# Batch 0's mirrored rows through device memory and gathers, its folds behind a chunk of batch 1: a lightning attention and Fourier mixing kernel

## The chip, the cores and the metric

The kernel runs on one core of a Trainium2 chip. Its time is the device time of one execution in microseconds. A core has five engines that run side by side, each with its own queue in a fixed order: TensorE (PE: matmuls and transposes into PSUM; its weight loads are shown as PEld), VectorE (DVE), ScalarE (ACT), GpSimd (POOL) and SyncE (SP), which here only starts DMAs. ACT and POOL start DMAs too.

## What is computed

Two stages, from the reference:

```
# attention, blocks of 64 positions, decay lam per head
intra = (qb @ kb.T * Dmask) @ vb
inter = (qb * lam_pow) @ kv_state
out[block] = intra + inter
kv_state = lam_block * kv_state + (kb * rev_pow).T @ vb
# bridge: x[b, s, h*D + d] = out[b, h, s, d]
mixed = real(fft(fft(x, axis=1), axis=2))
u = x + mixed
un = (u - mean(u)) / sqrt(var(u) + 1e-6)
result = u + relu(un @ w_ch1) @ w_ch2
```

There are 4 batches, 8 heads, 768 positions and 64 elements a head, so x has rows of 512 for each batch; w_ch1 is 512 x 2048 and w_ch2 2048 x 512. Both weights come as 64-bit floats and are converted on the chip.

## The kernel before

**Attention** (`attn`, L246) runs per batch over six chunks of 128 positions. `attn_in` (L259) loads q, k and v on SP's queue, multiplies k by the decay on POOL (kd, L270), transposes k and q on TensorE (L274, L279), copies them out on ACT and scales q on DVE (L285). `attn_out` (L289) forms the scores (L298), masks them on DVE (sc, L302), forms the state's increment (L315, then L319 on POOL and L320 on DVE) and the output transposed (L328, L332), which ACT copies to oT. The inner `back` (L345) transposes four tiles of it (L348) and copies two halves (L350, L351) to rows x, the second half of the columns reversed.

**Folds and Fourier.** The real part of the transform is made from sums and differences of row s and row S - s, so each batch needs its rows in mirrored order too. `fold_a` (L448) uses rows 384 to 576 and their mirror, `fold_b` (L452) the others; both are DVE work in place, the first two operations of each fold placed in program order on their engine (L418, L419). Then `fft_ln` (L483) runs the matmuls over the positions (L508), whose first one is placed in program order too, the matmuls over the width (L521 to L526), adds x, normalises (L534) and, for the first four groups, transposes the result to ut, the operand of the MLP. Groups of two row tiles are taken in the order 1, 2, 0.

**Mirrored rows.** There are two ways. For a batch in `TURNED`, only batch 0, `attn_out` copies the output with its positions reversed (L386; one column apart, L339, L341, L392), and `mirrored` (L374) passes it through `back` a second time. For the other batches x goes to two device memory tensors, xa and xb, on ACT's queue (L358, L360, L362), and `mirror_a` (L425, three gathers) and `mirror_b` (L441, two) fetch the rows in mirrored order by indirect DMAs from POOL.

**Order.** Every part is a Python generator that yields an estimate of its time; `weave`, `beside` and `part` interleave them, which gives the order in which the program is written. The framework's scheduler may move an instruction within its engine's queue from there. From L833 on: attention 0 runs with 8 of the 32 tiles of weights (each a load of 512 KB and five DVE and two ACT operations, L216 to L225); then the fold of batch 0 beside 2.5 chunks of attention 1; then the Fourier part of batch 0 beside 3.5 chunks and 4 weight tiles; then halves of the MLP (L625, L639) beside the rest of the weights and the fronts of batches 1 to 3. After 438 us of the profile come the last eight groups' products, joined in pairs (L712, L759). `LEADS = (0,)` lets attention 1 begin before batch 0's Fourier part.

Buffers that bear on it: x tiles of chunks 3 to 5 come from a pool of three (`xn`), those of chunks 0 to 2 and the mirrored tiles from one of twelve (`xp`), q, k and v from two each, PSUM tiles of the front from five.

Of the kernel before, what the change touches and what calls it, by code (L numbers as in the profile page):

```python
# [76 lines left out]
def kernel(  # L77
# [61 lines left out]
    def new(pool, shape, tag, **kw):  # L139
        cnt[0] += 1  # L140
        return pool.tile(shape, F32, tag=tag, name=f"{tag}{cnt[0]}", **kw)
# [87 lines left out]
    def weights():  # L229

        for h in range(2):
            for f in range(h * DFF // 2, (h + 1) * DFF // 2, WP):
                for c in range(KO):
                    load_weights(w1[:, c, f:f + WP], w1v[:, c, f:f + WP])
                    yield 1.0
            for c in range(h * FO // 2, (h + 1) * FO // 2):
                load_weights(w2[:, c, :], w2v[:, c, :])
                yield 1.0
# [7 lines left out]
    def attn(b):  # L246

        head = () if b - 1 in LEADS else attn_in(b, 0)
        for c in range(NC):
            yield from head  # L250
            head = attn_in(b, c + 1) if c < NC - 1 else attn_in(b + 1, 0) if b in LEADS else ()
            yield from attn_out(b, c, head)

    ins, oTs, eo = {}, {}, {}
    LEADS = (0,)
    TURNED = (0,)
    first = const.tile([128, HP, 1], F32, name="first")

    def attn_in(b, c):  # L259
# [29 lines left out]
    def attn_out(b, c, head):  # L289
# [45 lines left out]
        nc.scalar.copy(oT, po)  # L335
        if b in TURNED:

# [14 lines left out]

        if b not in TURNED:
            x = xn_[b, c] = new(xp, [C, DM], "x") if c < HC else new(xn, [C, DM], "xn")
# [126 lines left out]
    T_FOLD = 2 * (2 * 2.2 + 4 * 0.8)  # L481
# [314 lines left out]
    def weave(lead, other, ratio):  # L796

        t_lead = t_other = 0.0
        for d in lead:
            t_lead += d  # L800
            while t_other < t_lead * ratio:
                d = next(other, None)
                if d is None:
                    return t_lead + sum(lead)
                t_other += d
                yield d
            yield d
        return t_lead

    def run(gen):  # L810
        return sum(gen)

    def part(gen, n):
        for d in gen:
            yield d
            n -= d
            if n <= 0:
                return
# [5 lines left out]
    NW = 2 * KO * DFF // WP  # L824
    w = weights()
    t_chunk = 7.3
# [3 lines left out]
    def beside(lead, t, other, t_other):  # L830
        return weave(lead, part(other, t_other), t_other / t)

    att1, mix = attn(1), fft_ln(0)  # L833
# [1 line left out]
    run(part(att0, 2.7))  # L835
    run(beside(att0, NC * t_chunk - 2.7, w, 0.25 * NW))

    run(beside(part(mix, T_FOLD), T_FOLD, att1, 2.5 * t_chunk))
    run(beside(mix, 24.0, beside(att1, 3.5 * t_chunk, w, 0.12 * NW), 0.12 * NW + 2.5 * t_chunk))

    half = [[mlp(b, g, h * FO // 2, (h + 1) * FO // 2) for b, g in PLAIN[:3]] for h in range(2)]
    fr = chain([att1, fft_ln(1)] + [front(b) for b in range(2, B)])
# [52 lines left out]
```

## Time and profile before

| | |
|---|---|
| median of 6 runs | 831.65 us (830.02 to 833.84) |
| profiled execution | 831.25 us |
| its span, first to last instruction | 829.1 us |
| TensorE idle from 0 to 130 us | 20.6 us |
| mean granted TensorE clock | 0.996 |
| DMA moved | 68.87 MB |

All lines come from the profiled execution. A line of the timeline has the start and the length in us (or, for several merged, from the first to the last), the engine, the line of the source, the operation, what it writes and reads, and in brackets how long the engine was idle before and what it waited for. A q after an engine's name stands for its queue: the issue of a DMA, not its transfer. The chain of waits goes back from the last instruction to what released each step. Durations of single operations overlap by some 0.08 us on DVE and by more on TensorE, so in a full queue starts are closer than durations.

### The profile page before, as it was taken

What the parts mean: (1) busy time and instruction counts of PE and PEld (TensorE: products, weight loads), DVE (VectorE), ACT (ScalarE), POOL (GpSimd) and SP (SyncE); (2) the same over time, 40 slices, a digit from 0 to 9 for tenths busy, and PEclk for the clock granted to TensorE, in tenths of its full rate; (3) what the DMA queues carried; (4) which work ended last, traced back from release to release, by engine and by line L of the source; (5) the groups of instructions that cost most, each with busy time, mean ns of one, the idle gap of its engine ahead of it and who ended that gap; (6) DMA issues with size and microseconds to landing.
All of it is one profiled execution on the core that took longest, in us unless ns stands there. A gap on an engine that the chain in (4) does not pass through costs nothing.

```text
span 829.1 us, 11682 instructions
## 1 busy us (share of the span) xinstructions
PE 798.7 (96%) x4608; PEld 635.8 (77%) x4608; DVE 443.4 (53%) x1030; ACT 182.9 (22%) x436; POOL 79.1 (10%) x102
## 2 busy tenths in 40 slices
PE   6989889999999999999999999999999999999998
PEld 5767765758675857767748888888888888888886
DVE  6889788847943572355894551156313561145411
ACT  4755433215420210312102210022001210012100
POOL 3121140012110110220100000000000000000000
PEclk9999999999999999999999999999999999999999
DMA  9966633256950137430442011100111001100010
GB/s 248 257 148 179 165 110 98 72 135 169 248 150 27 51 61 156 115 132 3 115 123 80 1 52 51 51 1 0 52 51 51 0 1 39 33 32 1 1 39 25
DMA packets 126683, 68.87 MB, mean 83 GB/s; under 512 B 111150, under 2 KB 112174, under 8 KB 126630
## 3 DMA queue, kind: packets, MB, share of 16 engines
q1 hardware_dynamic: 121488, 55.67, 26.2%
q0 software_dynamic: 2112, 6.69, 2.4%
q10 hardware_dynamic: 3030, 5.78, 1.9%
q8 instruction: 36, 0.59, 0.3%
q14 instruction: 17, 0.14, 0.1%
HBM read 48.72 MB, written 19.40 MB: 82 GB/s over the span
## 4 chain that ended last, share of the span: by engine, by line
PE 80%; DVE 10%; issue 4%; DMA 3%; ACT 2%; POOL 1%; POOLq 0%; DVEq 0%; ACTq 0%
PE p L759 23%; PE p L712 23%; PE pm L639 10%; PE pm L625 7%; PE pa L508 3%; PE pa L332 3%; PE pa L298 3%; PE pa L328 2%; DMA x<-xb,ix 1%; PE pa L274 1%; PE pa L315 1%; PE pa L348 1%; DVE stt L538 1%; DMA xb<-xn 1%; PE pa L279 1%
## 5 line engine op out<-in xcount | busy, mean ns | idle before, releaser
L625 PE MATMUL pm<-ut,w 128*128 128x256 f32 x512 | 119.1, 382 | 0.2 <-DVE hr L631 0.2
L639 PE MATMUL pm<-w,hr 128*128 128x512 f32 x256 | 117.7, 604 | 1.3 <-DVE hr L631 1.3
L625 PEld LDWEIGHTS pm<-ut,w 128*128 128x128 f32 x512 | 94.4, 190 | 15.4 <-issue 3.1
L712 PE MATMUL p<-ur,w 128*128 128x256 f32 x384 | 93.8, 379 | 0.0
L639 PEld LDWEIGHTS pm<-w,hr 128*128 128x128 f32 x256 | 47.2, 192 | 51.3 <-issue 47.7
L712 PEld LDWEIGHTS p<-ur,w 128*128 128x128 f32 x384 | 73.0, 190 | 10.3 <-issue 0.5
L712 PE MATMUL p<-us,w1s 128*128 128x256 f32 x256 | 65.7, 379 | 0.0
L759 PE MATMUL p<-w,hs 128*128 128x256 f32 x256 | 58.0, 379 | 0.5 <-DVE y L780 0.5
L759 PE MATMUL p<-w2s,hs 128*128 128x256 f32 x256 | 57.9, 379 | 0.0
L759 PE MATMUL p<-w,ha 128*128 128x256 f32 x256 | 57.9, 379 | 0.0
L759 PEld LDWEIGHTS p<-w,hs 128*128 128x128 f32 x256 | 48.5, 190 | 7.5 <-DVE y L780 0.9
L759 PEld LDWEIGHTS p<-w2s,hs 128*128 128x128 f32 x256 | 48.6, 190 | 6.6
L712 PEld LDWEIGHTS p<-us,w1s 128*128 128x128 f32 x256 | 48.6, 190 | 6.6
L759 PEld LDWEIGHTS p<-w,ha 128*128 128x128 f32 x256 | 48.6, 190 | 6.6
L614 POOL DMA_INDIRECT out_dram<-y,ix x12 | 11.9, 988 | 408.1 <-DVE y L785 343.7
L739 ACT COPY ha<-p 128x256 f32<-128x256 f32 x32 | 11.9, 372 | 169.1 <-PE p L712 169.1
L332 PE MATMUL pa<-sc,v 128*64 128x128 f32 x384 | 32.3, 286 | 5.6 <-DVE sc L302 5.6
L750 DVE TENSOR_TENSOR ha<-p,ha 128x256 f32<-128x256 f32 x32 | 13.6, 425 | 44.8 <-ACT ha L749 44.8
L302 DVE TENSOR_TENSOR sc<-pa,decay 128x512 f32<-128x512 f32 x48 | 31.4, 683 | 11.0 <-PE pa L298 10.8
L298 PEld LDWEIGHTS pa<-qT,kT 64*128 64x128 f32 x384 | 26.1, 193 | 12.2 <-ACT qT L281 5.4
L332 PEld LDWEIGHTS pa<-sc,v 128*64 128x64 f32 x384 | 23.5, 140 | 14.5 <-DVE sc L302 9.5
L298 PE MATMUL pa<-qT,kT 64*128 64x128 f32 x384 | 30.8, 292 | 2.6 <-ACT qT L281 2.3
(144 smaller groups left out, 1133.2 us busy)
## 6 DMA issues: line engine op xcount, KB each, us to landing
raw<-in_moe_w_ch_dram SPq DMA_DIRECT2D x32, 512.0 KB, 4.9
k<-in_k_dram SPq DMA_DIRECT2D x24, 256.0 KB, 4.8
q<-in_q_dram SPq DMA_DIRECT2D x24, 256.0 KB, 5.0
v<-in_v_dram SPq DMA_DIRECT2D x24, 256.0 KB, 3.5
ud<-x SPq DMA_DIRECT2D x16, 256.0 KB, 2.3
utd<-e SPq DMA_DIRECT2D x64, 64.0 KB, 2.2
u<-ud SPq DMA_DIRECT2D x16, 256.0 KB, 2.7
ur<-utd SPq DMA_DIRECT2D x6, 512.0 KB, 4.3
```

The source lines that it names most:

```text
L298: mm(pss[hi][:, hp, :], lhsT=kT[HD[hi], hp, :], rhs=qT[HD[hi], hp, :], start=True, stop=True)
L302: nc.vector.tensor_tensor(t, pss[hi], decay[:, hi::2, :], op=ALU.mult)
L328: mm(po[HD[hi], hp, :], lhsT=s_old[HD[hi], hp, :], rhs=qs[HD[hi], hp, :], start=(hp == 0), stop=False, skip_group_check=True)
L332: mm(po[HD[hi], hp, :], lhsT=vt[:, 2 * hp + hi, :], rhs=sc[hi][:, hp, :], start=(c == 0 and hp == 0), stop=(hp == HP - 1), skip_group_chec ...
L508: mm = nc.tensor.matmul(ps[0:m, n, :], lhsT=piece(a, i, n), rhs=cs[0:rows, a, i in (2, 3), n, :], start=(a == 0), stop=(a == 1))
L614: nc.gpsimd.indirect_dma_start(out=out.rearrange("b s d -> (b s) d"), out_offset=row_of(2 + HC * (b + 1) + T - HC), in_=y[:, :], in_offset ...
L625: nc.tensor.matmul(ps, lhsT=w1[:, c, 128 * fc:128 * fc + 128], rhs=ut[:, c, :], start=(c == 0), stop=(c == KO - 1))
L639: nc.tensor.matmul(ps, lhsT=hr[(fc - f0) // 4][:, fc % 4, 128 * i:128 * i + 128], rhs=w2[:, fc, :], start=(fc == f0), stop=(fc == f1 - 1))
L712: nc.tensor.matmul(ps, lhsT=s2.A[a][:, kt, 128 * i:128 * i + 128], rhs=U[b][:, kt, :], start=(first and kt == 0), stop=(kt == 1), skip_gro ...
L739: nc.scalar.copy(a11, two(X))
L750: V.tensor_tensor(a22, two(Z), a22, op=ADD)
L759: nc.tensor.matmul(ps, lhsT=h[a][:, s, i, :], rhs=s2.B[b][:, i, :], start=(first and i == 0), stop=(i == HF - 1), skip_group_check=True)
```

## The change

`TURNED` becomes empty, so batch 0 takes the path of the others: no reversed copy, no second `back`, but writes to xa and xb and five gathers. Its first three gathers come after chunk 4's rows (L363), not placed in program order (`pin` is false there), and the last two after chunk 5. And the order after attention 0 is rewritten: first one chunk of attention 1 beside two weight tiles, then the fold beside two chunks, then the Fourier part beside three chunks and two weight tiles.

```diff
     LEADS = (0,)
-    TURNED = (0,)
+    TURNED = ()
...
-    run(beside(part(mix, T_FOLD), T_FOLD, att1, 2.5 * t_chunk))
-    run(beside(mix, 24.0, beside(att1, 3.5 * t_chunk, w, 0.12 * NW), 0.12 * NW + 2.5 * t_chunk))
+    run(beside(part(att1, t_chunk), t_chunk, w, 0.06 * NW))
+    run(beside(part(mix, T_FOLD), T_FOLD, att1, 2.0 * t_chunk))
+    run(beside(mix, 24.0, beside(att1, 3.0 * t_chunk, w, 0.06 * NW), 0.06 * NW + 2.5 * t_chunk))
```

## The prediction

> **What bounds the kernel now.** I began with the page's busy shares and slices. TensorE is busy 96% of the span, so nearly everything is a queue of matmuls, and a change can only act where that queue has holes.
>
> ```profile
> PE 798.7 (96%) x4608; PEld 635.8 (77%) x4608; DVE 443.4 (53%) x1030; ACT 182.9 (22%) x436; POOL 79.1 (10%) x102
> ...
> PE   6989889999999999999999999999999999999998
> ...
> DVE  6889788847943572355894551156313561145411
> ```
>
> The holes are in the first six slices (20.7 us each), and there VectorE, not TensorE, is dense. So I cut that stretch at its own events: the end of attention 0, the start of the second half of fold 0, its end, the first MLP operand.
>
> ```profile
> 0.00:47.00 47.00, 38.03 (x435) 30.77 (x436) 36.93 (x75) 27.80 (x59) 12.90 (x25) 1.00 1.00 243
> 47.00:52.00 5.00, 3.53 (x42) 2.59 (x40) 4.72 (x11) 3.05 (x9) 0.00 (x0) 1.00 0.77 157
> 52.00:56.50 4.50, 4.25 (x54) 3.19 (x51) 2.10 (x5) 2.25 (x5) 1.64 (x2) 1.00 0.15 36
> 56.50:72.60 16.10, 13.04 (x146) 10.10 (x144) 16.07 (x34) 5.67 (x13) 3.85 (x4) 0.90 0.65 172
> 72.60:94.40 21.80, 19.61 (x203) 16.03 (x203) 18.82 (x40) 10.55 (x24) 4.17 (x5) 0.99 0.58 154
> 94.40:110.20 15.80, 15.22 (x126) 13.01 (x125) 12.66 (x29) 8.01 (x20) 4.67 (x5) 1.00 0.67 184
> ```
>
> Columns: stretch, its length, busy us of PE, weight loads, DVE, ACT, POOL, then clock, DMA share, GB/s. From 56.5 to 72.6 DVE is busy 16.07 of 16.10 us: the folds set the pace while TensorE waits. From 94.4 on the first MLP operand exists and TensorE has filler. So what counts is when the first MLP operand is ready, and how much TensorE work is left then.
>
> Third, the chain of waits at the end of attention 0, where the mirrored rows are made:
>
> ```profile
> 47.39 0.59 ACT oT L335
> ...
> 48.10 0.67 PE pa L348 x4
> ...
> 48.79 0.37 ACT x L350
> ...
> 49.44 0.49 ACT ds L386
> ...
> 50.07 0.66 PE pa L348 x4
> 50.73 1.14 PE pa L298 x16
> ```
>
> The scores of batch 1's first chunk (L298) stand in TensorE's queue behind two rounds of reversed copy and transposition.
>
> Fourth, the same gathers as batch 1 does them, the nearest price for what is added:
>
> ```profile
> 111.20 0.33 ACTq L362 DMA_DIRECT2D xb<-xn  x1
> ...
> 114.45 3.77 POOL L444 DMA_INDIRECT x<-xb,ix  x1 [0.81 <-DMA xb<-xn]
> ...
> 118.52 0.95 POOL L444 DMA_INDIRECT x<-xb,ix  x1 [0.30 <-issue]
> ...
> 120.53 0.69 DVE L418 TENSOR_TENSOR fe<-x,x 128x512 f32<-128x512 f32 x1 [2.94 <-DMA x<-xb,ix]
> ```
>
> From the write's issue to the first fold that can use the rows: 120.53 - 111.20 = 9.3 us.
>
> **Part 1, what attention 0 loses and gains.** Mirrored rows go: `back` runs 6 times for batch 0, not 10. That is 16 transposes, 0.44 us of TensorE per four at the spacing they have in a full queue, 1.8 us; 8 half copies of about 0.4 us, 5 reversed copies of 0.60 and 6 small ones of about 0.17: 7.2 us of ACT. ACT gets 7 DMA issues (one row, four to xa, two to xb) at 0.25 to 0.66 us, about 2.6.
>
> At the tail I read the chain. Today 3.36 us pass from oT's start (47.37) to L298 (50.73). Without the rounds of reversal the scores need oT and qT, 0.59 + 0.59, so they start near 48.6: **-2.1**. In chunks 2 to 4 the same things lie inside (0.44 + 0.17 us each, at most 1.8 together), but DVE is busy 17.6 of 20 us from 20 to 40, so I take a third: **-0.6**, bounds 0 and -1.8.
>
> Against it stand the writes. Queue 10 needed 1.9% of 16 engines' span for 3030 packets, 83 ns each; one 256 KB tile is 128 packets, 0.66 us over 16 engines. Three fall before 40 us, where the DMA share is 0.99 to 1.13, and the next chunk's loads queue with them. Bounds 0 and +2.0, taken **+0.6**: the wait of the transposes for q there was only 0.4 us. Sum: the first score product of DVE (51.85 today) comes 2.1 earlier, at 49.75. If the cover of DVE work is stricter than I think, this term is nearer -1.
>
> **Part 2, fold 0 moves behind a chunk and two weights.** Read from the yields of the generators, the order in emission is now: chunk 0 of attention 1 with two weight tiles, the first half of fold 0, then its second half with two chunks. Costs on DVE, at the spacing of the rows: a fold's first half 3.9 us (eight operations from 47.06 to 51.6), a weight tile 0.34 + 0.34 + 0.33 + 0.60 + 0.60 = 2.2, a chunk's scores, state and scaled q 2.2. The first half today uses DVE while attention 0 ends, as the 47 to 52 row shows (4.72 of 5). Afterwards weights can use that slot, but it shrinks by the 2.1 saved, to 1.8; of two weight tiles (4.4) 2.6 are left. Chunk 0 today takes 4.7 us from its first product to scaled q (51.85 to 56.57), with 2.4 idle on DVE; the 2.6 fill that and add 0.2. So the fold starts at 49.75 + 4.9 = 54.65 and its first half ends at 58.55. The last rows of attention 0 are written from 49.35 (47.37 + oT 0.59 + transposes 0.7 + copies 0.7), so by the 9.3 of batch 1 they are folded from 58.65. The second half with its two chunks takes the 16.1 us that it has today and ends at 74.75, where today it is 72.63: **+2.1**. The Fourier matmuls follow it by the same distance.
>
> From there to the first MLP operand (21.8 us) there is one weight tile less, 2.2 us of DVE; DVE is busy 18.8 of 21.8 but the chain there is largely L508, so I take half: **-1.1**, bounds 0 and -2.2. After that TensorE has filler, and the rest shifts with it; a second weight tile less could give up to -1.0 there, taken 0, since TensorE is full at 15.2 of 15.8.
>
> Two things I cost at nothing. The two weight loads (issues of 0.4 to 0.8 us) now stand on SP's queue ahead of the loads for chunk 1; the DMA share of 0.15 from 52 hides them, else 1.6 us. Batch 0 now holds three xn buffers instead of two; batch 1's last chunk waits for one at 110.5 today already (on L601), and goes on waiting there.
>
> **Part 3, what is new on POOL.** Five gathers of 0.94 to 3.77 us stand in one queue with kd (L270) and the state decay (L319), and the two for xb wait for a write. Behind a waiting gather wait kd of chunk 1 or 2, behind it TensorE's L315, and everything behind L315. POOL is busy only 1.64 of the 4.5 us from 52, so some of it is hidden; if kd is issued first, all of it. Today kd of chunk 1 starts at 52.58, takes 1.06, and L315 runs at 56.99: 3.35 us of slack. Two gathers ahead of it with a wait (0.81 + 3.77 + 0.30 + 0.95 + 0.30 = 6.1) would make it 2.8 late. Also, Part 2 has no slack: each 1 us by which rows land later delays the fold by 1, with the fold's first operation placed in order on DVE, so that score products behind it wait too. Bounds 0 and +4, taken **+1.0**.
>
> The page "SBUF — State Buffer" of the Trainium skill, section "Who interferes with whom", says that tensor_tensor takes only the read interface of the port shared with GpSimd, so that descriptors are not held up, and that a two-port copy or tensor_scalar holds them only until it ends. The row of 3.77 us beside rows of 0.95 stood next to fold operations that are all tensor_tensor, with one scaling between; by the rule it should have cost at most about 0.7 more, by the row 2.8 more. By the rule the rows would land 2 us earlier and Part 3 would be near 0, by the row it stays.
>
> **The clock.** After the gaps of 58 to 70 us the granted clock was half:
>
> ```profile
> 70.00:72.00 2.00, 2.00 (x15) 1.67 (x12) 2.00 (x5) 0.69 (x2) 0.67 (x1) 0.50 0.01 1
> ```
>
> It cost 1.5 us (14 products at L332 1.90 for 1.03, eight at L508 2.12 for 1.51). The fold now has two chunks beside it instead of two and a half, so one such dip stays, taken 0; bounds -1.5 and +1.5.
>
> The page "TensorE: Matmul & The Clock Gate", section "What's actually happening", puts the drop after an idle window of some 3.4 us. No gap of that length stands before this dip (the longest waits were about 1.5 us), so by the rule the dip would not be there; by the row, short gaps in number suffice.
>
> **Sum.** -2.1 in attention is already inside the +2.1 at the fold's end; then -1.1 and +1.0: **+2.0 us**. The profiled execution took 831.25 us (span 829.1 and 2.15 around it), 0.4 below the median of the six runs, so 833.25 for it and **833.7** for a median. With every bound the good way, 1.2 + 0.6 + 1.1 + 1.0 + 1.0 + 1.5 = 6.4 us come off that, 827.3; the bad way 0.6 + 1.4 + 1.1 + 3.0 + 1.5 = 7.6 come on, 841.3.
>
> **Rivals.** A measurement here tells 0.2% (1.7 us) from no change.
> - *The removed work wins (faster).* DVE's work up to 110 us is unchanged, only reordered; weights fill the slots and come back one for one. Then the whole removed TensorE work (1.8) and some of the tail show: 831.65 - 2.5 = **829.2**. For it: DVE idle of 2.4 in 52 to 56.5 is there to be filled. Against: the fold lies on a chain that starts later.
> - *It cancels (same).* Instructions are already issued out of program order (today's first fold operation stands before a weight's last). If the fold is not really postponed, +2.1 is near 0 and the rest cancels: **831.7**.
> - *Rows land late (much slower).* One wait of DVE at the fold's second half like the 2.94 us of batch 1, here without an MLP to cover it, and TensorE cold after it (1.5): 833.7 + 4.4 = **838.1**. It decides once write and gathers take over 9.3 us. For it: the second row of 0.95 and landing times up to 6.5 us when loads run. Against: DMA share is only 0.15 from 52 to 56.5.
>
> **Chances.** Forecast 0.36 (own range 833.3 to 836.5); faster 0.34; same 0.20; rows late 0.10. So slower 0.46. The range 828.3 to 838.3 takes in both sides and leaves out the extremes of the added bounds.
>
> **What would show it.** Scores of batch 1's first chunk near 48.6; first fold operation near 54.7 and none before 50; first L508 near 73.7 (71.6 today); first MLP operand copied near 95.4 (94.4). Wrong if L508 starts before 72, or if kd waits behind a gather and L315 of chunk 1 with it. If total TensorE idle before 130 us (20.6 us today) falls, the faster rival holds.

## The result, and the profile after the change

| | before | changed |
|---|---|---|
| median | 831.87 us (70 runs) | 834.24 us (33 runs, 830.44 to 841.68) |
| ratio of changed to before | | 1.0045, 95% interval 1.0032 to 1.0058 |
| profiled execution, its span | 831.25, 829.1 us | 832.9, 830.9 us |
| TensorE busy, idle over the span | 798.7, 30.4 us | 797.5, 33.4 us |

By the ratio the change costs 0.45%, some 3.7 us of 831.65; the medians lie 2.4 us apart, the means of the runs 3.8 (835.13 against 831.37). In the two profiled executions TensorE has 1.2 us less to do and is idle 3.0 us longer: the span is 1.8 us longer.

The page of the changed kernel, the same three lines as before:

```profile
PE 797.5 (96%) x4592; PEld 635.8 (77%) x4592; DVE 443.9 (53%) x1030; ACT 178.1 (21%) x417; POOL 85.3 (10%) x107
...
PE   6868899999999999999999999999999999999998
...
DVE  6979589857843582245895551155312561145411
```

The 16 transposes and 19 ACT operations are gone, POOL has five gathers more. The third slice of TensorE (41 to 62 us) fell from 8 to 6, and DVE's fell there too. Now the same stretches in both kernels, from the view by windows (columns as in the prediction). The changed kernel:

```profile
46.00:60.00 14.00, 8.84 (x104) 7.58 (x102) 8.81 (x17) 6.74 (x14) 8.60 (x9) 0.88 1.14 297
60.00:74.00 14.00, 11.31 (x119) 8.97 (x120) 13.93 (x29) 4.74 (x10) 3.65 (x4) 0.88 0.61 149
...
110.00:130.00 20.00, 19.23 (x118) 14.22 (x118) 19.02 (x49) 8.14 (x19) 3.08 (x5) 1.00 0.36 111
0.00:130.00 130.00, 106.36 (x1021) 85.52 (x1022) 104.34 (x220) 56.41 (x118) 38.95 (x50) 0.95 0.76 202
```

The kernel before:

```profile
46.00:60.00 14.00, 11.01 (x138) 8.40 (x136) 11.32 (x22) 6.27 (x17) 2.84 (x3) 1.00 0.62 134
60.00:74.00 14.00, 12.20 (x112) 9.67 (x113) 13.96 (x31) 5.49 (x12) 2.65 (x3) 0.88 0.56 155
...
110.00:130.00 20.00, 15.98 (x60) 10.97 (x59) 16.13 (x44) 3.55 (x9) 5.73 (x4) 0.91 0.24 78
0.00:130.00 130.00, 109.45 (x1043) 86.48 (x1044) 107.23 (x230) 60.88 (x137) 32.96 (x45) 0.97 0.69 176
```

From 46 to 60 us TensorE loses 2.17 us of work, and what it does there it does partly at a lower clock (0.88). Two columns name the suspects: POOL rose from 2.84 to 8.60 us, the DMA share from 0.62 to 1.14. From 110 to 130 us TensorE is 3.25 us fuller than before: the wait of 3.05 us ahead of batch 1's first Fourier matmul, which ended at 124.00 before, is not in this trace. So part of the loss is given back late, and over 130 us 3.09 us of work are missing.

The chain of waits of the changed kernel at the start of attention 1 (start, length, engine, what it makes, line):

```profile
45.86 0.59 ACT oT L335
...
47.57 1.21 PE pa L298 x16
48.81 0.94 POOL fo L431
50.06 1.19 POOL x L437
51.27 1.07 POOL kd L270
52.39 0.94 PE pa L315 x16
53.33 1.72 PE pa L332 x16
```

Where two rounds of reversed rows stood, there are now two gathers and the multiplication of k by the decay. POOL's timeline of the same kernel shows why:

```profile
47.33 1.17 POOL L431 DMA_INDIRECT fo<-xa,ix  x1 [12.51 <-DMA xa<-xn]
48.81 0.94 POOL L431 DMA_INDIRECT fo<-xa,ix  x1 [0.31 <-PE pa L298]
50.06 1.19 POOL L437 DMA_INDIRECT x<-xa,ix  x1 [0.31 <-issue]
51.27 1.06 POOL L270 TENSOR_TENSOR kd<-k,decay 128x512 f32<-128x512 f32 x1
53.84 1.43 POOL L444 DMA_INDIRECT x<-xb,ix  x1 [1.50 <-DVE st L317]
55.57 0.95 POOL L444 DMA_INDIRECT x<-xb,ix  x1 [0.30 <-issue]
```

POOL stands idle for 12.51 us at a gather that waits for the rows in device memory. kd of batch 1's first chunk stands behind three gathers, though its k was there: TensorE transposes that k at 45.75 us. TensorE's L315 waits 3.65 us for kd (PE's timeline, changed kernel):

```profile
52.39 0.94 PE L315 MATMUL pa<-v,kd 128*64 128x64 f32 x16 [3.65 <-POOL kd L270]
```

In the kernel before, kd ran as soon as its k had landed, and L315 did not wait for it (timelines of POOL and PE):

```profile
43.29 1.17 POOL L270 TENSOR_TENSOR kd<-k,decay 128x512 f32<-128x512 f32 x1 [8.32 <-DMA k<-in_k_dram]
51.75 0.69 PE L315 MATMUL pa<-v,kd 128*64 128x64 f32 x16
```

The granted clock is halved after that wait (view by windows, changed kernel):

```profile
52.00:54.00 2.00, 1.61 (x26) 1.61 (x28) 0.63 (x2) 0.00 (x0) 0.49 (x2) 0.66 1.17 282
54.00:56.00 2.00, 2.00 (x15) 1.67 (x12) 2.00 (x5) 0.92 (x2) 1.70 (x2) 0.50 1.19 268
```

The second suspect shows on DVE, in its timeline (changed kernel):

```profile
53.37 0.42 DVE L317 COPY st<-pa 128x256 f32<-128x256 f32 x1 [2.65 <-PE pa L315]
...
56.88 1.58 DVE L220 TENSOR_TENSOR e<-e 128x512 bf16<-128x512 bf16 x1 [0.85 <-ACT e L218]
58.39 0.68 DVE L224 SCALAR_TENSOR_TENSOR w<-raw,w 128x512 f32<-128x512 uint32 x1
59.10 0.69 DVE L225 SCALAR_TENSOR_TENSOR w<-w,e 128x512 f32<-128x512 f32 x1
...
60.31 1.07 DVE L418 TENSOR_TENSOR fe<-fo,xn 128x512 f32<-128x512 f32 x1
```

The last operation of the second weight tile ends just before the scaled q, and the fold's first operation, which is placed in program order, comes after both: at 60.31, not 54.65.

### The profile page after: what moved, and what is told of

It reads as the page before. It is cut to its first block, busy times and chain, and to the rows that moved or that the text cites. A ratio compares the mean times of both kernels' runs of the same rounds, so it can differ in the third digit from the quotient of the medians.

```text
span 830.9 us, 11646 instructions
## 1 busy us (share of the span) xinstructions
PE 797.5 (96%) x4592; PEld 635.8 (77%) x4592; DVE 443.9 (53%) x1030; ACT 178.1 (21%) x417; POOL 85.3 (10%) x107
## 4 chain that ended last, share of the span: by engine, by line
PE 78%; DVE 12%; issue 4%; DMA 3%; POOL 1%; ACT 1%; SPq 0%; POOLq 0%; DVEq 0%; ACTq 0%
PE p L759 23%; PE p L712 23%; PE pm L639 10%; PE pm L625 7%; PE pa L508 3%; PE pa L298 2%; PE pa L332 2%; PE pa L328 1%; DVE stt L538 1%; PE pa L274 1%; DVE un L556 1%; PE pa L315 1%; DVE sc L302 1%; DVE x L591 1%; DMA x<-xb,ix 1%
## 5 line engine op out<-in xcount | busy, mean ns | idle before, releaser
L759 PEld LDWEIGHTS p<-w,ha 128*128 128x128 f32 x256 | 48.6, 190 | 6.6
L759 PEld LDWEIGHTS p<-w2s,hs 128*128 128x128 f32 x256 | 48.6, 190 | 6.6
L712 PEld LDWEIGHTS p<-us,w1s 128*128 128x128 f32 x256 | 48.6, 190 | 6.6
L298 PEld LDWEIGHTS pa<-qT,kT 64*128 64x128 f32 x384 | 25.5, 195 | 14.9 <-ACT qT L281 8.3
L298 PE MATMUL pa<-qT,kT 64*128 64x128 f32 x384 | 30.4, 293 | 5.0 <-ACT qT L281 5.0
```

What stands on the lines that cost most here:

```text
L298: mm(pss[hi][:, hp, :], lhsT=kT[HD[hi], hp, :], rhs=qT[HD[hi], hp, :], start=True, stop=True)
L712: nc.tensor.matmul(ps, lhsT=s2.A[a][:, kt, 128 * i:128 * i + 128], rhs=U[b][:, kt, :], start=(first and kt == 0), stop=(kt == 1), skip_gro ...
L759: nc.tensor.matmul(ps, lhsT=h[a][:, s, i, :], rhs=s2.B[b][:, i, :], start=(first and i == 0), stop=(i == HF - 1), skip_group_check=True)
```

## The experiments

Four facts had to be told apart: POOL's order, the two weight tiles (their loads and their DVE work), the traffic of the writes, and the new order of the fold itself. Each kernel was timed in five rounds beside the kernel before on the same chip. The table gives the ratio to it, below 1 is faster; "kd first" and "weights late" are explained below it. The medians are of 11 or 12 runs, for e3 of 6 and for e9 of 7. Traces show one execution each: e1's profiled one was the fastest of its twelve (829.07 us), e3's the slowest of its six (840.39).

| label | based on | edit | median, us | ratio, 95% interval |
|---|---|---|---|---|
| e1_kd_first | changed | kd first | 831.28 | 1.0017 (0.9990 to 1.0043) |
| e5_kd_first_again | changed | kd first | 831.81 | 1.0002 (0.9982 to 1.0023) |
| e2_order_only | changed | mirrored rows on the chip as before | 834.07 | 1.0034 (1.0014 to 1.0054) |
| e3_path_only | before | gathers, old order | 838.22 | 1.0087 (1.0057 to 1.0116) |
| e4_writes_only | before | the writes alone, unread | 831.67 | 0.9998 (0.9980 to 1.0016) |
| e6_kd_first_w_late | changed | kd first, weights late | 828.42 | 0.9961 (0.9941 to 0.9981) |
| e12_kd_first_w_late_again | changed | the same | 827.52 | 0.9947 (0.9931 to 0.9963) |
| e7_order_w_late | e2 | weights late | 833.15 | 1.0012 (0.9993 to 1.0031) |
| e8_kd1_first | changed | kd of chunks 0 and 1 first | 831.14 | 0.9985 (0.9968 to 1.0002) |
| e9_kd1_first_w_late | e8 | weights late | 827.28 | 0.9948 (0.9929 to 0.9968) |
| e10_after_w_late | changed | weights late | 831.38 | 0.9994 (0.9982 to 1.0007) |
| e11_path_kd_first | e3 | kd first | 834.87 | 1.0036 (1.0015 to 1.0057) |

### kd ahead of the gathers

The three gathers of batch 0 are called in its last chunk, after the head of attention 1 has been written, and placed in program order:

```diff
-            if c == NC - 2 and b - 1 not in LEADS:
+            if c == NC - 2 and b - 1 not in LEADS and b not in LEADS:
                 mirror_a(b)
             elif last:
+                if b in LEADS:
+                    mirror_a(b, pin=True)
                 mirror_b(b)
```

> Batch 0's first three gathers are written behind kd of batch 1's first chunk, in program order. Queue theory (kd of that chunk stands on POOL behind gathers that wait for xa; TensorE waits 3.65 us at L315 and then runs at half clock): that wait is gone, chunk 0's L315 starts near 49 instead of 52.4, the first L508 near 74, and the time falls by 2.5 to 5 us from the changed kernel's 834.2, to 829.5 to 832. Order theory (the fold behind a chunk and two weight tiles is what costs): the wait goes, but the time stays at 833 to 835. Traffic theory (the writes and gathers load the DMA queues before 50 us): 833 to 835 as well.

POOL's timeline of e1_kd_first:

```profile
43.10 1.06 POOL L270 TENSOR_TENSOR kd<-k,decay 128x512 f32<-128x512 f32 x1 [9.46 <-DMA k<-in_k_dram]
45.44 1.18 POOL L433 DMA_INDIRECT fo<-xa,ix  x1 [1.28 <-DMA xa<-xn]
...
53.08 1.06 POOL L446 DMA_INDIRECT x<-xb,ix  x1 [3.93 <-DMA xb<-xn]
```

kd runs at 43.10 as soon as k is there, the gathers follow, and L315 of chunk 0 runs at 47.79 without a wait. The ratio falls from 1.0045 to 1.0017. But TensorE is not full in its place; it meets another wait, for the load of q of chunk 1:

```profile
54.01 0.63 PE L279 MATMUL pa<-ident,q 128*128 128x128 f32 x4 [2.17 <-DMA q<-in_q_dram]
```

This q landed 9.34 us after its issue. The same kernel again:

> The first experiment's kernel once more. Queue theory: 830 to 832.5 again, 2 to 3 us under the changed kernel's 834.2. If it was a chance of that chip, 833.5 to 835.

It gave 1.0002; the two average 1.001 (e1's interval still overlaps that of the changed kernel, e5's does not). So kd behind the gathers costs some 0.35%, 3 us, and without it the changed kernel is about level with the one before. In e5's trace the wait for q is longer and k is late too (PE's timeline of e5_kd_first_again):

```profile
52.29 0.63 PE L274 MATMUL pa<-ident,k 128*128 128x128 f32 x4 [1.55 <-DMA k<-in_k_dram]
56.56 1.08 PE L279 MATMUL pa<-ident,q 128*128 128x128 f32 x4 [3.64 <-DMA q<-in_q_dram]
```

The first fold operation comes at 58.91 us there, at 55.90 in e1: one kernel, two executions. A single event time is no finer than this.

### The order alone, the gathers alone

`TURNED = (0,)` in the changed kernel leaves the new order with the mirrored rows made on the chip; `TURNED = ()` in the kernel before does the opposite.

```diff
 # e2_order_only, on the changed kernel
-    TURNED = ()
+    TURNED = (0,)
 # e3_path_only, on the kernel before
-    TURNED = (0,)
+    TURNED = ()
```

> The kernel before with the changed order alone; mirrored rows still made on chip. Queue theory: no gathers for batch 0, no wait of L315 on kd; the time is that of before or a little off it, 831 to 833. Order theory: the first L508 near 75 instead of 71.6 and 833.5 to 836. Traffic theory: 831 to 832.5.

> The kernel before with batch 0's rows through device memory and gathers, in the old order. Queue theory: L315 of batch 1's first chunk waits on kd as in the changed kernel, and the fold, first in order, waits on DVE for the gathers besides: 834 to 838. Order theory: no later fold, 831 to 833. Traffic theory: as the changed kernel, 833.5 to 835.

The order alone costs 0.34%, the gathers alone 0.87%, together they cost 0.45%: they are no sum. e2_order_only came out as the order theory had it (834.07 us, first L508 at 74.60). In e3_path_only L315 waits 3.2 us for kd as in the changed kernel, and then DVE waits too, for rows that are still on their way when the old order comes to the fold (timeline, and the view by windows):

```profile
52.50 0.69 DVE L418 TENSOR_TENSOR fe<-fo,xn 128x512 f32<-128x512 f32 x1 [4.67 <-DMA fo<-xa,ix]
```
```profile
48.00:60.00 12.00, 5.58 (x52) 4.48 (x52) 6.73 (x11) 1.35 (x4) 8.15 (x8) 0.65 0.85 212
```

TensorE does 5.58 us of work in 12 and the clock falls to 0.65. The changed kernel's DVE waits for no gather from 44 to 80 us: the fold stands later there. In e12_kd_first_w_late_again (below), where only the chunk stands ahead of the fold, DVE waits for no gather either, so the chunk is enough. With kd put first in the old order as well (the diff of e1_kd_first on e3_path_only):

> The third experiment (gathers in the old order) with kd of chunk 0 ahead of the gathers. Queue theory: L315's wait of 3.2 us goes, and the time falls from 838.2 by 2 to 4, to 834 to 836; DVE still waits at the fold's first operation for the gathers (4.7 us there), so it does not reach 832. If the wait for the rows is nearly all of that price: 837 to 839.

838.22 became 834.87. The wait for kd is gone, and DVE still waits for the rows at the fold's first operation (timeline of e11_path_kd_first):

```profile
51.82 0.69 DVE L420 TENSOR_TENSOR fe<-fo,xn 128x512 f32<-128x512 f32 x1 [5.33 <-DMA fo<-xa,ix]
```

The old order with gathers stays slower than the kernel before.

### The writes alone

Six of the seven writes of batch 0's rows to xa and xb are added to the kernel before, and nothing reads them:

```diff
             back(oT, x)
+            if c == 0:
+                xd[b] = (dram.tile([S - 256, DM], F32, name=f"xa{b}"), dram.tile([257, DM], F32, name=f"xb{b}"))
+                nc.scalar.dma_start(xd[b][1][256:257], x[0:1])
+            else:
+                nc.scalar.dma_start(xd[b][0][(c - 1) * C:c * C], x)
+            if c == NC - 2:
+                nc.scalar.dma_start(xd[b][1][0:C], x)
             yield 1.7
```

> The kernel before with six of batch 0's seven writes to xa and xb added, which nothing reads. Traffic theory: loads of k, q, v and weights land later, 833 to 835. Queue and order theories: 831 to 832.5, within 0.2% of before.

0.9998, interval 0.9980 to 1.0016: their traffic and ACT's issues cost nothing that can be told, within some 1.5 us. The traffic of the gathers themselves was not tried alone.

### The two weight tiles

The changed kernel runs two weight tiles beside attention 1's first chunk, ahead of the fold. "Weights late" puts them beside the Fourier part:

```diff
-    run(beside(part(att1, t_chunk), t_chunk, w, 0.06 * NW))
+    run(part(att1, t_chunk))
     run(beside(part(mix, T_FOLD), T_FOLD, att1, 2.0 * t_chunk))
-    run(beside(mix, 24.0, beside(att1, 3.0 * t_chunk, w, 0.06 * NW), 0.06 * NW + 2.5 * t_chunk))
+    run(beside(mix, 24.0, beside(att1, 3.0 * t_chunk, w, 0.12 * NW), 0.12 * NW + 2.5 * t_chunk))
```

Alone, on the changed kernel:

> The changed kernel with the two weight tiles back in the Fourier part, kd still behind the gathers. If the two prices add: 831 from the changed kernel's 834.2, ratio 1.000 to 1.002, with the wait of L315 on kd still 3 to 4 us. If the kd wait hides the weights' cost (DVE works on them while TensorE stands): 833.5 to 834.5, ratio 1.003 to 1.005.

0.9994, from 1.0045: the two tiles cost about 0.5%, 4 us (the medians differ by 2.9). kd of chunk 0 still stands behind the three gathers, and the wait for it is still there (timeline and windows of e10_after_w_late):

```profile
51.10 0.69 PE L315 MATMUL pa<-v,kd 128*64 128x64 f32 x16 [3.12 <-POOL kd L270]
```
```profile
46.00:60.00 14.00, 10.33 (x122) 8.21 (x122) 5.71 (x11) 3.65 (x9) 9.06 (x9) 0.88 0.98 240
```

DVE has 3.1 us less to do there than in the changed kernel, TensorE 1.5 us more, and the first fold operation comes at 56.95 instead of 60.31. One thing more moved: kd of chunk 1 now stands ahead of the last two gathers (51.94 us; 57.12, behind them, in the changed kernel), so the 4 us may hold some of that. Together with kd first, in two kernels of the same text:

> The same, and the two weight tiles beside batch 1's first chunk go back to the Fourier part. Order theory in its weights' half (two tiles, 4.4 us of DVE and 1 MB of loads, stand before the fold): the fold's first operation comes 1.5 to 3 us earlier than the 55.9 of the first experiment, q of chunk 1 is not 2.17 us late, and the time falls by 1 to 3 us, to 828.5 to 830.5. If the DVE work is only moved: 831 to 832.

> The sixth experiment's kernel once more: 827.5 to 829.5, ratio 0.994 to 0.998, if its gain over both kernels is real; 831 to 832.5 if it was chance.

0.9961 and 0.9947: both intervals lie below 1, and this version beats both kernels. The two edits taken one by one give 0.35% and 0.51%, together 0.91% (1.0045 less the mean of 0.9954): two prices that add. Where the time comes from (view by windows of e12_kd_first_w_late_again):

```profile
46.00:60.00 14.00, 13.06 (x173) 10.44 (x172) 10.16 (x18) 6.08 (x14) 8.97 (x9) 1.00 1.20 269
...
0.00:130.00 130.00, 110.47 (x1048) 87.42 (x1049) 107.46 (x232) 56.70 (x120) 43.06 (x50) 0.97 0.77 198
```

From 46 to 60 us TensorE does 13.06 us of work at full clock, against 8.84 in the changed kernel and 11.01 before, although the DMA share is as high as in the changed kernel (1.20). The weight tiles also stand in SP's queue ahead of other loads. DMA issues on SP in the changed kernel:

```profile
42.52 1.50 SPq L209 DMA_DIRECT2D raw<-in_moe_w_ch_dram  x2
44.11 0.46 SPq L263 DMA_DIRECT2D k<-in_k_dram  x1
46.40 0.38 SPq L263 DMA_DIRECT2D q<-in_q_dram  x1
```

and in e12_kd_first_w_late_again:

```profile
42.12 0.83 SPq L263 DMA_DIRECT2D k<-in_k_dram  x1
43.05 1.11 SPq L263 DMA_DIRECT2D q<-in_q_dram  x1
```

These are the loads of chunk 1 of attention 1: k goes 2.0 us and q 3.3 us earlier. Not all of it is the weights: in e1, with the weights still ahead, k goes at 43.48 and q at 44.54, so against e1 it is 1.4 and 1.5 us. The traces say where the loads matter. With kd first, TensorE waits for k and q of chunk 1 (3.1 us in e1, 5.2 in e5), and with the weights late these waits are gone (e6, e12). With kd behind the gathers TensorE waits for no load of that chunk, in the changed kernel or in e10, so there the price does not come through such a wait; the DVE work ahead of the fold and the place of kd of chunk 1 remain. How the 4 us divide was not measured.

The same edit with the rows made on the chip:

> The changed order with on-chip mirrored rows, the two weight tiles going back to the Fourier part; so only the chunk stands before the fold. If the weights were the order's price: back to 831.5 to 832.5, first fold operation near 56.5 instead of 59.4. If the chunk is: 833.5 to 835.

1.0012, against 1.0034 without the edit. The intervals overlap, so what the weights cost there is not settled; its trace does not help, as the first fold operation comes at 59.69 us, behind an attention 0 that ends 3 us later than before at a granted clock of 0.88 from 20 to 30 us. Against it, 0.9954 with the gathers and the same order says that the path through device memory, once nothing waits behind it, is worth some 0.6% (0.9954 against 1.0012), about 5 us.

### kd of the second chunk first as well

The last two gathers are called in attention 1's second chunk, after its kd:

```diff
             nc.gpsimd.tensor_tensor(kd, kt, kpow, op=ALU.mult)
+        if b - 1 in LEADS and c == 1:
+            mirror_b(b - 1, pin=True)
...
```

> As the first experiment, and the two gathers from xb are written behind kd of chunk 1. Queue theory taken further (kd of chunk 1 stood behind gathers until 56.0): L315 of chunk 1 no later than 55.5 instead of 57.3, the time 0 to 2 us under the first experiment's; but the fold's second half may wait for rows that land later, then 0 to 2 us over it. Traffic theory (q of chunk 1 landed 9.3 us after its issue, and that is what chunk 1 waited for): no gain, within 0.1% of the first experiment.

> Both gains together: all of batch 0's gathers behind kd of chunk 0 or 1, and the two weight tiles back in the Fourier part. If both are separate prices: 827 to 829, ratio 0.994 to 0.997. If kd of chunk 1 is not the limit once the weights are gone (in the sixth experiment it already ran at 50.4, ahead of the gathers from xb): the same as the sixth, 0.996 within 0.002.

0.9985 and 0.9948. The first is better than the mean of e1 and e5 (1.001) by less than the intervals tell, the second equals e6 and e12. In e12_kd_first_w_late_again, which does not ask for it, kd of chunk 1 stands ahead of the last two gathers anyway (49.76 and 52.48 us). Why the framework places it so once the weights are late was not looked into.

## Why the prediction was right, and where its steps were not

It forecast slower, 833.7 us; the median is 834.24. That the end came out so near is luck in good part: the fold and the first MLP operand came more than 5 us later than predicted, and a gain that the sum did not hold made up for it. The steps one by one, with events of one profiled execution each:

| event, us | before | predicted | changed | kd first (e1) | both (e12) |
|---|---|---|---|---|---|
| scores of batch 1's chunk 0 (L298) | 50.66 | 48.6 | 47.57 | 46.70 | 46.98 |
| first fold operation (L418) | 47.06 | 54.65 | 60.31 | 55.90 | 52.80 |
| end of fold 0 | 72.63 | 74.75 | 80.00 | 76.27 | 72.91 |
| first L508 | 71.55 | 73.7 | 75.39 | 72.09 | 68.73 |
| second copy to ut | 94.39 | 95.4 | 101.66 | 96.81 | 94.29 |

- **Part 1, the tail and the chunks: right, and larger than taken.** L298 comes 3.1 us earlier. From oT's start (47.39 before, 45.86 now) to L298 3.3 us became 1.7, a gain of 1.6 against 2.1 taken; the other 1.5 us were gained in the chunks before, where the terms were -0.6 and, for the writes, +0.6: net -1.5 instead of 0. What the writes took of it is not shown. e4_writes_only bounds their cost in the whole time to some 1.5 us, and in its trace attention 0 ends 2.5 us late at a clock of 0.83 from 20 to 30 us, which e7, without such writes, shows too (0.88).
- **Part 3, POOL: the mechanism right, the chunk and the size wrong.** "Behind a waiting gather wait kd of chunk 1 or 2" was, in the trace, kd of chunk 0, and the prediction took +1.0 out of 0 to +4. e1 and e5 against the changed kernel, and e6 and e12 against e10, put it at 0.35 to 0.4%, 3 us. Its sentence "if kd is issued first, all of it" is what e1 shows for the wait on kd; the cure uncovered the wait for q. "Wrong if ... kd waits behind a gather and L315 of chunk 1 with it" was the prediction's own sign, and it came true one chunk earlier.
- **Part 2, the step that failed: "Two things I cost at nothing. The two weight loads ..."** The cover named was the DMA share of 0.15 from 52 us on. It was read in the wrong place and from the wrong kernel. In the wrong place, because the weight loads go out at 42.52 us and those of chunk 1 went at 41.62 and 42.83 in the kernel before, where the share was 0.92 (40 to 47 us). From the wrong kernel, because batch 0's writes and gathers were not in it: from 52 to 56.5 us the share is 0.31 with the new order alone (e2) and 1.20 in the changed kernel. Put late, the two tiles are worth 0.5%, about 4 us, with all that follows from their place: their loads, the 4.4 us of DVE work ahead of the fold, and the place of kd of chunk 1. The prediction filled DVE's holes with that work (it counted 0.2 us) and gave 1.1 back for it later, which did not come: from the fold's end to ut it is 21.7 us, 21.8 before. The fold began at 60.31, 5.7 us after the time predicted. Either edit alone brings it forward, to 55.90 or 58.91 with kd first (e1, e5) and to 56.95 with the weights late (e10), and both together to 52.80 (e12). In the changed kernel the wait for kd also left DVE without work from 50.7 to 53.4.
- **The sum: every microsecond of ut counted whole, the path's gain at nothing.** "After that TensorE has filler, and the rest shifts with it" made the shift of the first MLP operand the change of the time. ut came 7.3 us later and the span is 1.8 longer. Among kernels of one path this measure holds: in the eight traces with gathers and the new order, from e9 to the changed kernel, the second copy to ut moves from 93.31 to 101.66 us and the span from 824.5 to 830.9, in nearly the same order. Between the two paths it does not. In e12 ut comes as in the kernel before (94.29 and 94.39), and the span is 4.0 us shorter, 2.6 of it less TensorE work and 1.4 less idle time. The prediction had the removed TensorE work (1.8 us) only in a rival, not in its sum; e7 against e6 and e12 puts the path's gain at some 5 us. The wait at 124 us went with the old order: one of 3.0 to 3.1 us before batch 1's first Fourier matmul is in all four traces of the old order (before, e3, e4, e11) and in none of the new.
- **The test by TensorE's idle total.** The idle total before 130 us, which the prediction named as the test for the faster rival, went the right way (20.6 us before, 23.6 in the changed kernel, 19.5 in e12), but it is no better measure across kernels: it is 22.7 in e1 at a span of 827.0 and 19.0 in e7 at 832.6, where TensorE's busy time itself is longer (802.9 us, 799.0 in e2, for the same 4608 matmuls).
- **Rivals.** *The removed work wins* does not hold for this change, yet holds for its repaired form: 828.0 between e6 and e12, where it said 829.2. *It cancels* described the changed kernel with kd first (1.001). *Rows land late* was not seen: no wait of DVE on a gather from 44 to 80 us, and batch 0's gathers took 0.94 to 1.43 us in the changed kernel, none 3.77. That the mechanism is real e3_path_only shows, where the order that the change replaces waits 4.67 us for rows.
- **The clock: a term taken as 0.** One dip was to stay; the changed kernel has two before 74 us, at 52 to 56 and 62 to 66, and its mean over 130 us is 0.95 against 0.97. The price of the second was not separated. The longest wait before the dip at 70 us in the kernel before was 1.26 us (59.96), not 1.5.
- **The port.** The prediction kept a row of 3.77 us against the rule of the Trainium skill's page "SBUF — State Buffer" ("Who interferes with whom"), by which tensor_tensor does not hold descriptors up. No gather of batch 0 came near it in any trace (at most 1.43 us). Among batch 1's two gathers from xb, though, one took 2.0 to 3.5 us in nine of the twelve experiments, so the long row was no accident. Beside the row of 3.77 us DVE ran more than one scaling, contrary to the prediction's reading (L556 at 115.26, L631 at 117.18). What makes these long was not tried.

Left open: how the weights' price divides into loads, DVE work and the place of kd of chunk 1, how the new order removes batch 1's wait at 124 us, and whether an order exists in which the rows made on the chip do as well as e12.

## What to carry to other kernels

A gather that waits for a write held what stood behind it in its engine's queue (here POOL stood for 12.51 us), so a computation that others need at once belongs ahead of it; look for what was put last on an engine that seems 90% idle. A cover for a new load must be read at the time when that load goes out, and from the kernel as it will be: the transfers that a change adds can use up the idle share that was to hide its other loads. The time of one early event can rank kernels that share a path, as ut did here; between two paths, the work taken off the engine that is full needs a term of its own in the sum.

## What the runs showed of the hardware

- **Half clock after short gaps.** The changed kernel has a second dip (view by windows):

```profile
62.00:64.00 2.00, 1.24 (x8) 0.85 (x10) 2.00 (x6) 0.00 (x0) 0.00 (x0) 0.72 0.23 50
64.00:66.00 2.00, 2.00 (x16) 1.67 (x13) 1.97 (x4) 0.59 (x1) 0.93 (x1) 0.50 0.00 0
```

  The gaps of TensorE from 57 to 63 us are 0.85, 0.91 and 1.13 us. The Trainium skill's page "TensorE: Matmul & The Clock Gate" ("What's actually happening") has the clock drop after an idle window of some 3.4 us. The dip at 52 to 56 us, after 3.65 us, agrees; this one, and the one before at 70 us, do not, if the window is read as one unbroken gap. Here three gaps with 2.9 us in sum stood before the dip. But the sum of short gaps alone does not decide it either: e12 has gaps of 1.81, 0.46, 0.25 and 0.68 us from 60 to 67 us, 3.2 in sum, and its granted clock stays at 1.00 until 74 us. What decides was not found.
- **POOL or DVE operations that took longer side by side.** In the changed kernel kd took 2.64 us at 76.74 and the state decay 3.48 us at 81.74, while DVE ran mostly two-input operations; they took 1.06 and 0.63 us at 57.12 and 56.54. At 57.12 it was the other way round: kd kept its 1.06 us, and DVE's L220 beside it took 1.58 us, against 0.42 at 54.31. Neither was isolated.
- **A load can take 9.34 us** (q, 256 KB) where the share of the DMA engines is above 1 (1.13 from 46 to 60 us in e1_kd_first; 1.11 from 40 to 60).
